# Attention and expert layers on one core: another order of the first loads, and identity multiplications in the first batch's attention

## The chip, the cores and the metric

The kernel runs on one core of a Trainium2 chip. The metric is the device time of one execution in microseconds (us). Engines are named as the profile names them: PE is TensorE (PEld its weight loads), DVE is VectorE, ACT is ScalarE, POOL is GpSimd, SP is the engine whose queue issues nearly all DMAs.

## The reference

```python
def sm_attn(qq, kk, vv):                       # softmax(q k^T / 8) v, row maximum subtracted
    s = scale * np.matmul(qq, kk.transpose(0, 1, 3, 2))
    ...
    return np.matmul(a, vv)
p_packed = sm_attn(p, k, v)                    # 32 packed queries per head, over 576 keys
out = sm_attn(q, p_packed, p_packed)           # 576 queries per head, over the 32 packed rows
# x = out with heads side by side: 4608 tokens x 512
p = domain_probs / (domain_probs.sum(-1, keepdims=True) + 1e-09)
for e in range(4):                             # w1[e] is 512 x 1024, w2[e] is 1024 x 512
    out += p[:, e:e + 1] * (np.maximum(x @ w1[e], 0.0) @ w2[e])
```

There are 8 batches of 8 heads with head dimension 64, all in float32; q, k and p are drawn eight times wider than usual.

## The kernel before

The expert layers are the bulk. Their 4096 hidden columns are cut into 8 chunks `ch` of 512. A unit (`units`, L332) is one chunk for one batch; there are 64, and the first four are chunk 0 and chunk 1 of batch 0, then chunk 0 and chunk 1 of batch 1. Each unit has a first product (hidden values, `mm1_part` and `mm1_evict`) and a second, which takes seven block products (`product`, in the order of `ORDER`) in place of eight. Between them DVE forms sums of blocks (`sblk`, L592), and every operand is split in a high part, which ACT casts, and a low part, which POOL subtracts (`s_operand`: tiles `st`, L110 and L114). The weights w2 of a chunk are split in the same way into seven pairs `tt` by `t_form` (sums at L633; casts and subtractions again at L110 and L114), are stored to DRAM (`td`, L610) and are loaded back for later batches (L606). A product needs the high and the low part of both its operands.

The attention output of a batch, split into `xh` and `xl`, is the moving operand of the first product. w1 is not multiplied with it directly: the packed values `ppbd` are folded into w1 first (`g_form`, and for batch 0 `folded`; operands `wraw`), and the result, split again, is `ghl`.

The start runs a path of its own for batch 0. Two `pack_unit` generators, one for each half `g` of the heads, make the packed values: scores of p and k (`scores`), row maximum and exponential, five transposes (L74), the products with v, one transpose of the result `ppn`, and copies to `ppbd`. Then `first_tokens` makes the scores of the 576 queries (operands `ppbd` and `kt`, here the tile of q), starts the fold of w1, does the softmax of the two halves in DVE and ACT, turns it (`turn`) and begins the first products. `fill` puts plain multiplications of the 128x128 identity by itself on PE, whose result is never read; there is one row of three, between the fold and the turn. `form` takes one step of `forms`, the generator that splits w2's chunk 0, and ties its cast to a place on ACT.

Batch 1's attention (`second`) runs between the products of units 0 and 1. Its last step is `xl` (POOL, L114), two of them, one for each half. Unit 2's first product needs both.

Within an engine the order is made by a scheduler from the order in which the code issues, except where `after` and `then` add an edge without a wait. SP issues DMAs strictly in its order, and an issue that waits holds all behind it.

Of the kernel before, what the change touches and what calls it, by code (L numbers as in the profile page):

```python
# [36 lines left out]
NPROD = len(ORDER)  # L37
FILL = (3,)


@with_exitstack
def attention_moe(ctx: ExitStack, tc: tile.TileContext, q, k, v, p, dp, w1, w2, out):
# [30 lines left out]
    def tr(**kw):  # L73
        on_pe(nc.tensor.transpose(**kw))  # L74
# [52 lines left out]

    def scores(bs, g, stationary, moving):

        pss = {b: dbl() for b in bs}  # L130
        calls = []
        for c in range(2):
            for j in range(2):
                for hh in range(2):
                    for b in bs:
                        p0 = 2 * j * NPK + cols(b, hh).start
                        calls.append(dict(
                            out=pss[b][p0:p0 + NPK, c, 0:HS], lhsT=stationary(b, 2 * g + j, hh),
                            rhs=moving[b][hh * D:(hh + 1) * D, j, c * HS:(c + 1) * HS], start=True, stop=True,
                        ))  # L140
        together(calls)
        return pss
# [6 lines left out]

    def pack_unit(bs, g, new, relief=False):  # L150
        nfull = S // P
# [19 lines left out]
        yield  # L171
        pss = scores(bs, g, lambda b, pr, hh: pts[b][hh * D:(hh + 1) * D, pr, :], kts)
        a1s, rss = {}, {}
# [24 lines left out]
        for b in bs:  # L198
            if b != bs[0]:
                vt = load_v(b)  # L200
            at = new(b, [P, len(SC), P], "at")
            ps = dbl()
            for c in range(nfull):
                tr(out=ps[:, 0, c * P:(c + 1) * P], in_=a1s[b][:, c * P:(c + 1) * P], identity=ident)
# [18 lines left out]
            yield  # L223
            ps = dbl()
            tr(out=ps[0:D, 0, 0:P], in_=ppn, identity=ident)
            psv = ps[0:D, 0, 0:P].rearrange("p (j n) -> p j n", j=2)
# [179 lines left out]
    def first_tokens(pools, qts, raws, forms, grps):  # L406
# [101 lines left out]
        last["ACT"] = marks["turned", b, 1]  # L508
        form()
        largest(0)  # L510
# [4 lines left out]
        scaled(0)  # L515
        form()
        form()
        spare = turned[0][:, 0, cut:cut + P]
        fill(FILL[0], spare)
        for g in range(NG):  # L520
            then("ACT", hi_of(ghls[g][:, 0, :], fold[:, g, :], nc.scalar))
        parts = turn(0)
        for g in range(NG):
            less(fold[:, g, :], ghls[g][:, 0, :])
        shifted(1)
        (t0, x0), (t1, x1) = parts
        then("DVE", hi_of(xh[:, 0, t0], x0, nc.vector))
        then("ACT", hi_of(xh[:, 0, t1], x1, nc.scalar))
        powers(1)
        for g in range(NG):  # L530
# [51 lines left out]
    def s_operand(u, i):  # L582

        name = ORDER[i] if u < LAST else PLAIN[i]
        blk = lambda n: blocks[u, n]
        if name[0] == "s":
            t = hpool.tile([P, 2, HS], F32, name="sblk", bufs=3)
            x, y, op = {
                "s1": ("a21", "a22", ALU.add), "s2": ("s1", "a11", ALU.subtract),
                "s3": ("a11", "a21", ALU.subtract), "s4": ("a12", "s2", ALU.subtract),  # L590
            }[name]
            marks["sum", u, name] = nc.vector.tensor_tensor(out=t, in0=blk(x), in1=blk(y), op=op).ins  # L592
            blocks[u, name] = t
        src = blk(name)
        st = st_tile(F32R)
        parts = hi_of(both(st, 0), src, nc.scalar).ins, lo_of(both(st, 1), src, both(st, 0), nc.gpsimd).ins
        for ins, prev in zip(parts, marks.get("operand", ())):
            after(ins, prev)
        marks["operand"] = parts
        blocks[u, "op", i] = st  # L600

# [12 lines left out]
    def t_form(ch, new, eng):  # L614
# [3 lines left out]
        for name, shape in (("b11", [P, 2, DH]), ("b12", [P, 2, DH]), ("b2", [P, 2, DM])):  # L618
            blk[name] = new(shape, name)
            r0 = hf * FC + (0 if name != "b2" else 2 * P)  # L620
            c0 = DH if name == "b12" else 0
            nc.sync.dma_start(
                out=blk[name], in_=w2[e, r0:r0 + 2 * P, c0:c0 + shape[2]].rearrange("(f p) d -> p f d", p=P),
            )
        blk["b21"], blk["b22"] = blk["b2"][:, :, 0:DH], blk["b2"][:, :, DH:DM]
        yield
# [146 lines left out]
    with ExitStack() as first:  # L773
# [5 lines left out]
        def form_tile(shape, name):  # L779
            if name == "b2":  # L780
                return st_tile(F32)[:, 0:2 * DM].rearrange("p (f d) -> p f d", f=2)
            return hpool.tile(shape, F32, name="ablk", bufs=6)

        packs = [pack_unit([0], g, unit_tile(g)) for g in range(NG)]
        forms = t_form(0, form_tile, {n: nc.gpsimd for n in ("t1", "t2", "t3", "t4")})
        norm_probs()
        for i in (0, 1, 0, 1):
            next(packs[i])
        loads = first_loads()
        qts = [next(loads)]  # L790
        next(forms)
        qts.append(next(loads))
        raws = w1_load(0)
        load_probs(0, 0)
# [18 lines left out]
    after(mm1_evict(0, *rest), marks["sum", 0, "s3"])  # L813
    drain(forms)

# [29 lines left out]
    for u, (sb, ch, b) in enumerate(units):  # L845
# [44 lines left out]
        for i in range(NPROD):  # L890
            product(u, i)
            if (u, i) == (0, 0):
# [3 lines left out]
                for raw, ghl in lows:  # L896
                    nc.scalar.copy(out=ghl[:, 1, :], in_=raw)
            n = i + LA
# [76 lines left out]
```

## Time and profile before

| | us |
|---|---|
| median of 3 runs (1280.68 to 1282.36) | 1282.11 |
| the profiled execution | 1287.0 |
| its span, first to last instruction | 1285.2 |
| PE busy in the span | 1264.0 (98%) |
| DVE / POOL / ACT busy | 955.6 / 859.9 / 492.0 |

The profile is of one execution. Busy PE time counts from the start of a matmul to its modelled end, so rows that overlap add up to more than the stretch they stand in, and a PE that is busy all the time can still be slow: its clock can be granted at half. [...] A multiplication of two float32 operands is two records in the profile, a transpose is one.

### The profile page before, as it was taken

The page shows a single profiled execution, that of the slowest core. Times are in us where ns is not written, and L with a number is a line of the kernel's source. Part 1 is how long each engine was busy: PE and PEld are TensorE (multiplying, and loading weights), DVE is VectorE, ACT ScalarE, POOL GpSimd, SP SyncE. Part 2 cuts the span into 40 slices and gives each one's busy share as a digit, 9 for nine tenths or more (in the row PEclk, how much of TensorE's full clock was granted, in tenths as well). Part 3 has the DMA queues.
Part 4 walks back from the last instruction along what each step waited for, and adds up shares of the span by engine and source line. Part 5 has one row for each costly group of instructions (what it writes and reads, how often), then busy time and mean ns, then how long its engine had stood idle before and what let it go on. Part 6 is the DMA issues. An engine that isn't in the chain of part 4 may idle for free.

```text
span 1285.2 us, 26859 instructions
## 1 busy us (share of the span) xinstructions
PE 1264.0 (98%) x10762; PEld 1177.1 (92%) x10762; DVE 955.6 (74%) x1299; ACT 492.0 (38%) x888; POOL 859.9 (67%) x570
## 2 busy tenths in 40 slices
PE   7999999999999999999999999999999999999998
PEld 5789998998999999999999999999999999999998
DVE  4686777899985666998677667799679567766776
ACT  2644535646335333333334423333333533332321
POOL 2878889798995455666578454476668755556565
PEclk7999999999999999999999999999999999999999
DMA  8896656545465444555355646434446443343563
GB/s 300 306 319 221 203 176 224 168 162 184 159 216 201 145 159 141 189 167 157 115 145 173 200 143 196 137 132 132 144 138 203 149 143 117 125 157 125 176 219 100
DMA packets 91707, 223.93 MB, mean 174 GB/s; under 512 B 9280, under 2 KB 32192, under 8 KB 91584
## 3 DMA queue, kind: packets, MB, share of 16 engines
q1 hardware_dynamic: 90768, 221.92, 52.2%
q8 instruction: 86, 1.41, 0.5%
q10 hardware_dynamic: 816, 0.30, 0.1%
q14 instruction: 37, 0.30, 0.1%
HBM read 183.31 MB, written 38.87 MB: 173 GB/s over the span
## 4 chain that ended last, share of the span: by engine, by line
PE 70%; POOL 15%; DVE 8%; issue 3%; DMA 2%; ACT 2%; SPq 0%; ACTq 0%; POOLq 0%; DVEq 0%
PE dbl L69 63%; POOL st L114 9%; PE dbl L79 6%; POOL tt L114 2%; DVE sblk L592 2%; POOL acc L743 2%; DVE ghl L114 1%; DVE acc L712 1%; DVE ablk L363 1%; POOL xl L114 1%; PE dbl L74 1%; DMA tt<-td 1%; ACT ghl L110 1%; POOL b L633 0%; DVE a L250 0%
## 5 line engine op out<-in xcount | busy, mean ns | idle before, releaser
L69 PE MATMUL dbl<-st,tt 128*128 128x288 f32 x5388 | 765.1, 296 | 4.3 <-DVE ghl L114 1.4
L69 PEld LDWEIGHTS dbl<-st,tt 128*128 128x128 f32 x5388 | 723.3, 188 | 49.1 <-issue 26.1
L114 POOL TENSOR_TENSOR st<-sblk,st 128x576 fp32r<-128x576 f32 x252 | 396.5, 1581 | 231.8 <-ACT st L110 227.0
L69 PE MATMUL dbl<-xh,ghl 128*128 128x288 f32 x2016 | 409.0, 295 | 2.2 <-DVE ghl L114 2.1
L114 POOL TENSOR_TENSOR st<-ablk,st 128x576 fp32r<-128x576 f32 x193 | 293.1, 1522 | 138.4 <-ACT st L110 133.2
L712 DVE TENSOR_TENSOR acc<-dbl,acc 128x576 f32<-128x576 f32 x385 | 287.5, 750 | 101.8 <-PE dbl L69 101.4
L69 PEld LDWEIGHTS dbl<-xh,ghl 128*128 128x128 f32 x2016 | 322.4, 188 | 3.0 <-DVE ghl L114 2.9
L363 DVE SCALAR_TENSOR_TENSOR ablk<-dbl,pbt 128x576 f32<-128x576 f32 x256 | 192.1, 752 | 141.3 <-PE dbl L69 138.9
L69 PE MATMUL dbl<-xl,ghl 128*128 128x288 f32 x1008 | 296.3, 295 | 0.2 <-POOL xl L114 0.2
L110 ACT CAST st<-sblk 128x576 fp32r<-128x576 f32 x252 | 170.2, 676 | 277.0 <-DVE sblk L592 222.3
L110 ACT CAST st<-ablk 128x576 fp32r<-128x576 f32 x193 | 130.2, 675 | 252.2 <-PE dbl L69 221.5
L69 PEld LDWEIGHTS dbl<-xl,ghl 128*128 128x128 f32 x1008 | 188.9, 188 | 0.5 <-POOL xl L114 0.5
L592 DVE TENSOR_TENSOR sblk<-ablk 128x576 f32<-128x576 f32 x126 | 134.9, 1071 | 9.6 <-DVE ablk L363 0.5
L110 ACT CAST ghl<-dbl 128x512 fp32r<-128x512 f32 x128 | 72.6, 587 | 117.9 <-PE dbl L79 60.1
L114 DVE TENSOR_TENSOR ghl<-dbl,ghl 128x512 fp32r<-128x512 f32 x124 | 83.3, 686 | 20.5 <-ACT ghl L110 18.5
L592 DVE TENSOR_TENSOR sblk<-ablk,sblk 128x576 f32<-128x576 f32 x63 | 77.5, 1230 | 5.4
L79 PE MATMUL dbl<-wraw,ppbd 64*32 64x512 f32 x1024 | 69.9, 604 | 0.0
L114 POOL TENSOR_TENSOR tt<-b,tt 128x512 fp32r<-128x512 f32 x42 | 62.8, 1504 | 2.1 <-ACT tt L110 2.0
L592 DVE TENSOR_TENSOR sblk<-sblk,ablk 128x576 f32<-128x576 f32 x63 | 57.6, 915 | 1.3
L743 POOL TENSOR_TENSOR acc<-acc,acc 128x576 f32<-128x576 f32 x28 | 43.4, 1561 | 12.5 <-DVE acc L712 12.5
L710 ACT COPY acc<-dbl 128x576 f32<-128x576 f32 x56 | 35.8, 640 | 36.8 <-PE dbl L69 36.8
L79 PEld LDWEIGHTS dbl<-wraw,ppbd 64*32 64x32 f32 x1024 | 15.3, 106 | 21.6 <-issue 19.2
(117 smaller groups left out, 474.3 us busy)
## 6 DMA issues: line engine op xcount, KB each, us to landing
tt<-td SPq DMA_DIRECT2D x192, 512.0 KB, 4.3
wraw<-in_w SPq DMA_DIRECT2D x136, 256.0 KB, 3.6
td<-tt SPq DMA_DIRECT2D x56, 512.0 KB, 3.9
pbt<-pnd SPq DMA_DIRECT2D x32, 288.0 KB, 4.0
out<-acc SPq DMA_DIRECT2D x31, 288.0 KB, 2.4
kt<-in_k SPq DMA_DIRECT2D x14, 576.0 KB, 5.6
kt<-in_q SPq DMA_DIRECT2D x14, 576.0 KB, 5.6
vt<-in_v SPq DMA_DIRECT2D x15, 512.0 KB, 5.4
```

The source lines that it names most:

```text
L69: res = nc.tensor.matmul(**kw)
L74: on_pe(nc.tensor.transpose(**kw))
L79: ins = nc.tensor.matmul(**kw).ins
L110: return nc.scalar.copy(out=dst, in_=src)
L114: return eng.tensor_tensor(out=dst, in0=src, in1=hi.bitcast(F32), op=ALU.subtract)
L363: res = nc.vector.scalar_tensor_tensor(out=a, in0=ps[:, :, 0:HS], scalar=0.0, in1=pbt[b][:, c * HS:(c + 1) * HS].rearrange("p (o t) -> p o ...
L592: marks["sum", u, name] = nc.vector.tensor_tensor(out=t, in0=blk(x), in1=blk(y), op=op).ins
L710: nc.scalar.copy(out=accs[b, i], in_=psv)
L712: nc.vector.tensor_tensor(out=accs[b, i], in0=psv, in1=accs[b, i], op=ALU.add)
L743: eng.tensor_tensor(out=m[dst], in0=m[x], in1=m[y], op=op)
```

## The change

First loads: SP loads both halves of q, then w1's chunk 0, then w2's chunk 0; before, w2's blocks stood between the first q and w1. w2's chunk 1 is now issued behind w1's chunk 1. w2's largest block (`b2`) of chunk 0 gets a tile of its own instead of borrowing one of the operand tiles.

Identity multiplications: nine ahead of the first scores of batch 0, two and four ahead of the transposes of its two halves, one ahead of each transpose of `ppn`; in `first_tokens` the row of three becomes a row of four ahead of the fold's correction by the high part (`less`), two ahead of the turn, which now comes behind that correction, and two ahead of the next correction.

Forms: of the seven steps that split w2's chunk 0, three are taken ahead of the first product and four behind the low parts of `ghl` in unit 0; before, all seven were taken ahead of the first product.

```diff
-FILL = (3,)
+FILL = (4, 2, 2)
+WARM = (9, 0, 2, 4, 0, 0, 1, 1)
...
+    def idle(ps, n):
+        return [dict(out=ps, lhsT=ident, rhs=ident, start=True, stop=True) for i in range(n)]
...
-        calls = []
+        calls = idle(pss[bs[0]][:, 1, HS:HS + P], fill)
...
+            if fill[1]:
+                together(idle(ps[:, 1, P:2 * P], fill[1]))
...
+            if fill[3]:
+                together(idle(ps[:, 1, 0:P], fill[3]))
...
-        form()
         largest(0)
...
-        form()
-        form()
-        spare = turned[0][:, 0, cut:cut + P]
-        fill(FILL[0], spare)
+        spare = accum[grps[0]][:, 1, HS:HS + P]
+        fill(FILL[0], turned[0][:, 0, cut:cut + P])
         for g in range(NG):
             then("ACT", hi_of(ghls[g][:, 0, :], fold[:, g, :], nc.scalar))
-        parts = turn(0)
         for g in range(NG):
             less(fold[:, g, :], ghls[g][:, 0, :])
+        form()
+        fill(FILL[1], turned[0][:, 0, cut:cut + P])
+        parts = turn(0)
         shifted(1)
...
+        fill(FILL[2], spare)
         powers(1)
...
+        if (u, i) == (0, 3):
+            after(parts[0], marks["lows"])
...
+            if ch == 1:
+                after(load.ins, marks["w1", 1])
...
-                return st_tile(F32)[:, 0:2 * DM].rearrange("p (f d) -> p f d", f=2)
+                return wpool.tile(shape, F32, name="b2")
...
-        loads = first_loads()
-        qts = [next(loads)]
+        qts = list(first_loads())
+        raws = w1_load(0)
         next(forms)
-        qts.append(next(loads))
-        raws = w1_load(0)
...
-    drain(forms)
...
                 for raw, ghl in lows:
-                    nc.scalar.copy(out=ghl[:, 1, :], in_=raw)
+                    last["ACT"] = nc.scalar.copy(out=ghl[:, 1, :], in_=raw).ins
+                marks["lows"] = last["ACT"]
+                for _ in forms:
+                    then("ACT", marks["form"])
...
-    nc = bacc.Bacc("TRN2", target_bir_lowering=False, num_devices=1)
+    nc = bacc.Bacc("TRN2", target_bir_lowering=False, num_devices=1, dynamic_dma_scratch_size=1024)
```

On PE the program starts so before (`kt,pt` are the scores of p and k, `ident,a` the transposes, `ppbd,kt` the scores of the queries, `wraw,ppbd` the fold, `ident,kt` the turn):

```order
L79 MATMUL dbl<-kt,pt 32x288 x16
L74 MATMUL dbl<-ident,a_215 128x128 x4
L74 MATMUL dbl<-ident,a_215 64x128
L74 MATMUL dbl<-ident,a_233 128x128 x4
L74 MATMUL dbl<-ident,a_233 64x128
L69 MATMUL dbl<-vt,at 32x64 x16
L69 MATMUL dbl<-vr,at 32x64 x4
L69 MATMUL dbl<-vt,at 32x64 x16
L69 MATMUL dbl<-vr,at 32x64 x4
L74 MATMUL dbl<-ident,ppn 64x128 x2
L79 MATMUL dbl<-ppbd_85,kt 128x64 x20
L79 MATMUL dbl<-wraw,ppbd_85 32x512 x8
```

and so with the change (the line numbers are its own):

```order
L80 MATMUL dbl<-ident 128x128 x9
L80 MATMUL dbl<-kt,pt 32x288 x16
L80 MATMUL dbl<-ident 128x128 x2
L75 MATMUL dbl<-ident,a_224 128x128 x4
L75 MATMUL dbl<-ident,a_224 64x128
L80 MATMUL dbl<-ident 128x128 x4
L75 MATMUL dbl<-ident,a_242 128x128 x4
L75 MATMUL dbl<-ident,a_242 64x128
L70 MATMUL dbl<-vt,at 32x64 x16
L70 MATMUL dbl<-vr,at 32x64 x4
L70 MATMUL dbl<-vt,at 32x64 x16
L70 MATMUL dbl<-vr,at 32x64 x4
```

Fifteen identity multiplications stand around the first batch's scores and transposes where there were none; two more follow, one ahead of each transpose of `ppn`.

On POOL the rows ahead of the first operand's low part are these before (`tt` the low parts of w2's chunk 0, L633 sums of w2's blocks, `st` low parts of product operands):

```order
L114 TENSOR_TENSOR tt<-ablk,tt 128x512
L633 TENSOR_TENSOR ablk<-ablk 128x512
L633 TENSOR_TENSOR ablk<-st_191,ablk 128x512
L114 TENSOR_TENSOR tt<-ablk,tt 128x512 x2
L633 TENSOR_TENSOR ablk<-st_191,ablk 128x512
L114 TENSOR_TENSOR tt<-ablk,tt 128x512
L633 TENSOR_TENSOR ablk<-ablk,st_191 128x512
L114 TENSOR_TENSOR tt<-ablk,tt 128x512
L114 TENSOR_TENSOR tt<-st_191,tt 128x512 x2
L114 TENSOR_TENSOR st_501<-ablk,st_501 128x2x288
```

and these with the change:

```order
L115 TENSOR_TENSOR tt<-ablk,tt 128x512
L646 TENSOR_TENSOR ablk<-ablk 128x512
L646 TENSOR_TENSOR ablk<-b_201,ablk 128x512
L115 TENSOR_TENSOR tt<-ablk,tt 128x512 x2
L646 TENSOR_TENSOR ablk<-b_201,ablk 128x512
L115 TENSOR_TENSOR st_515<-ablk,st_515 128x2x288
L115 TENSOR_TENSOR st_522<-sblk,st_522 128x2x288
L115 TENSOR_TENSOR st_568<-sblk,st_568 128x2x288
L115 TENSOR_TENSOR tt<-ablk,tt 128x512
```

Four low parts of w2's chunk 0 and one sum of its blocks have moved behind the first operand's low part.

Further on, POOL reaches batch 1's `xl` before over these rows (`a` is batch 1's softmax):

```order
L114 TENSOR_TENSOR st_997<-ablk,st_997 128x2x288
L114 TENSOR_TENSOR st_1019<-sblk,st_1019 128x2x288
L114 TENSOR_TENSOR tt<-b_523,tt 128x512
L114 TENSOR_TENSOR st_1066<-ablk,st_1066 128x2x288
L276 TENSOR_TENSOR a_852<-a_852,s_938 128x576
L114 TENSOR_TENSOR xl_807<-at,xh_806 128x576 x2
```

and with the change over these:

```order
L646 TENSOR_TENSOR b_527<-b_527,b_531 128x512
L115 TENSOR_TENSOR st_1088<-ablk,st_1088 128x2x288
L285 TENSOR_TENSOR a_874<-a_874,s_960 128x576
L115 TENSOR_TENSOR xl_829<-at,xh_828 128x576
L115 TENSOR_TENSOR tt<-b_527,tt 128x512
L115 TENSOR_TENSOR tt<-b_531,tt 128x512 x2
L115 TENSOR_TENSOR xl_829<-at,xh_828 128x576
```

Between the second operand's low part and the first `xl`, both included, POOL has 25 instructions before and 27 with the change. Three low parts of w2's chunk 1 now stand between the two `xl`.

## Rows read from the trace of the kernel before

**Rows 1.** The page: engines' share of the span, and the chain by engine.

```profile
PE 1264.0 (98%) x10762; PEld 1177.1 (92%) x10762; DVE 955.6 (74%) x1299; ACT 492.0 (38%) x888; POOL 859.9 (67%) x570
...
PE 70%; POOL 15%; DVE 8%; issue 3%; DMA 2%; ACT 2%; SPq 0%; ACTq 0%; POOLq 0%; DVEq 0%
```

**Rows 2.** Windows: PE, PEld, DVE, ACT, POOL busy, granted clock, DMA share, GB/s.

```profile
5.00:10.00 5.00, 4.42 (x37) 2.00 (x37) 1.51 (x5) 0.83 (x2) 0.00 (x0) 1.00 1.05 336
10.00:15.00 5.00, 3.67 (x87) 2.58 (x86) 1.92 (x7) 2.19 (x5) 1.12 (x1) 0.73 1.07 380
15.00:20.00 5.00, 4.84 (x25) 4.28 (x22) 1.15 (x5) 0.00 (x0) 2.68 (x3) 0.50 1.04 384
20.00:25.00 5.00, 5.00 (x27) 4.78 (x30) 1.85 (x3) 1.73 (x3) 1.36 (x2) 0.50 1.04 394
25.00:30.00 5.00, 5.00 (x26) 1.95 (x18) 4.31 (x6) 1.07 (x2) 2.39 (x2) 0.57 0.53 155
30.00:35.00 5.00, 3.70 (x23) 2.96 (x23) 2.66 (x5) 3.03 (x7) 0.77 (x1) 1.00 0.88 253
...
55.00:60.00 5.00, 5.00 (x106) 4.47 (x106) 2.95 (x6) 2.25 (x4) 5.00 (x4) 1.00 0.29 71
...
100.00:1285.00 1185.00, 1174.34 (x9990) 1105.17 (x9988) 892.91 (x1190) 448.26 (x806) 796.06 (x521) 1.00 0.50 163
```

**Rows 3.** Timeline of PE: start, length, engine, line, operands, records, wait before.

```profile
5.26 3.90 PE L79 MATMUL dbl<-kt,pt 64*32 64x288 f32 x32 [5.26 <-DMA kt<-in_k]
9.48 0.74 PE L74 MATMUL dbl<-ident,a 128*128 128x128 f32 x5 [0.33 <-ACT a L187]
...
12.24 1.08 PE L69 MATMUL dbl<-vt,at 128*32 128x64 f32 x32
...
13.62 1.08 PE L69 MATMUL dbl<-vt,at 128*32 128x64 f32 x32
...
16.01 8.77 PE L79 MATMUL dbl<-ppbd,kt 128*128 128x64 f32 x40
24.70 3.64 PE L79 MATMUL dbl<-wraw,ppbd 64*32 64x512 f32 x16
28.27 1.43 PE L79 MATMUL dbl<-ident 128*128 128x128 f32 x6
29.54 0.95 PE L79 MATMUL dbl<-ident,kt 128*128 128x128 f32 x5
...
41.01 1.92 PE L79 MATMUL dbl<-wraw,ppbd 64*32 64x512 f32 x16
...
45.10 1.17 PE L79 MATMUL dbl<-xh,pt 64*32 64x288 f32 x16
...
52.02 1.25 PE L74 MATMUL dbl<-ident,a 128*128 128x128 f32 x10
...
56.38 0.65 PE L69 MATMUL dbl<-vt,at 128*32 128x64 f32 x32
...
57.21 0.65 PE L69 MATMUL dbl<-xl,kt 128*32 128x64 f32 x32
```

**Rows 4.** Timeline of ACT, the high parts of the fold.

```profile
28.44 1.07 ACT L110 CAST ghl<-dbl 128x512 fp32r<-128x512 f32 x2 [4.36 <-PE dbl L79]
```

**Rows 5.** Timeline of POOL, from the second operand's low part to both `xl`.

```profile
44.74 2.79 POOL L114 TENSOR_TENSOR st<-sblk,st 128x576 fp32r<-128x576 f32 x2 [1.47 <-ACT st L110]
...
62.22 1.27 POOL L114 TENSOR_TENSOR tt<-b,tt 128x512 fp32r<-128x512 f32 x1 [1.28 <-ACT tt L110]
...
81.69 1.43 POOL L114 TENSOR_TENSOR xl<-at,xh 128x576 fp32r<-128x576 f32 x1
84.72 1.43 POOL L114 TENSOR_TENSOR xl<-at,xh 128x576 fp32r<-128x576 f32 x1 [1.60 <-ACT xh L110]
```

**Rows 6.** Timeline of PE around the first `xl`.

```profile
83.18 0.40 PE L69 MATMUL dbl<-xl,ghl 128*128 128x288 f32 x1 [0.24 <-POOL xl L114]
...
90.52 1.92 PE L79 MATMUL dbl<-wraw,ppbd 64*32 64x512 f32 x16
```

More of the change, by code (lines that the diff above doesn't have):

```diff
@@ L126, in norm_probs, with scores @@
         nc.scalar.dma_start(out=pnd.rearrange("e (p t) -> p e t", p=P), in_=pb)
-    def scores(bs, g, stationary, moving):
+    def idle(ps, n):
+        return [dict(out=ps, lhsT=ident, rhs=ident, start=True, stop=True) for i in range(n)]
+    def scores(bs, g, stationary, moving, fill=0):
         pss = {b: dbl() for b in bs}
-        calls = []
+        calls = idle(pss[bs[0]][:, 1, HS:HS + P], fill)
         for c in range(2):
@@ L148, in behind_w1, with pack_unit @@
             after(res.ins, marks["w1", 1])
-    def pack_unit(bs, g, new, relief=False):
+    def pack_unit(bs, g, new, relief=False, fill=(0, 0, 0, 0)):
         nfull = S // P
@@ L171, in pack_unit @@
         yield
-        pss = scores(bs, g, lambda b, pr, hh: pts[b][hh * D:(hh + 1) * D, pr, :], kts)
+        pss = scores(bs, g, lambda b, pr, hh: pts[b][hh * D:(hh + 1) * D, pr, :], kts, fill[0])
         a1s, rss = {}, {}
@@ L621, in t_form @@
             c0 = DH if name == "b12" else 0
-            nc.sync.dma_start(
+            load = nc.sync.dma_start(
                 out=blk[name], in_=w2[e, r0:r0 + 2 * P, c0:c0 + shape[2]].rearrange("(f p) d -> p f d", p=P),
             )
+            if ch == 1:
+                after(load.ins, marks["w1", 1])
         blk["b21"], blk["b22"] = blk["b2"][:, :, 0:DH], blk["b2"][:, :, DH:DM]
@@ L780, in form_tile @@
             if name == "b2":
-                return st_tile(F32)[:, 0:2 * DM].rearrange("p (f d) -> p f d", f=2)
+                return wpool.tile(shape, F32, name="b2")
             return hpool.tile(shape, F32, name="ablk", bufs=6)
-        packs = [pack_unit([0], g, unit_tile(g)) for g in range(NG)]
+        packs = [pack_unit([0], g, unit_tile(g), fill=WARM[g::NG]) for g in range(NG)]
         forms = t_form(0, form_tile, {n: nc.gpsimd for n in ("t1", "t2", "t3", "t4")})
```

## The prediction

> **What bounds the kernel now.** I read the page's shares and its chain first: PE is busy for 98% of the span and holds 70% of the chain, POOL 15% [rows 1]. So a microsecond counts only where PE stands still, runs slowly or does work it needn't. The windows came next, for the clock. From 100 us on PE is busy for 1174.3 of 1185.0 us at full clock, and the change leaves the order there nearly as it was, so nothing is to be had there [rows 2]. [...] In 30 to 35 us it was busy for 3.70 of 5 us and kept the full clock [rows 2].
>
> The scores of k ran at half speed too, whatever the window shows there: 32 records in 3.90 us, while 16 records of the same shape take 1.17 us later [rows 3].
>
> Then I read the timeline of POOL from the second operand's low part on, because PE waits for POOL at 83.18 us, for the first `xl` [rows 5, 6]. POOL is busy without a break in 55 to 60 us [rows 2], and from 44.74 to the end of that `xl` at 83.12 its only long wait that I found is the 1.28 us at 62.22 [rows 5]. There POOL and PE finish together. This place decides what an earlier start is worth.
>
> **The front, part by part.** I add up how much earlier PE starts the turn (29.54 before) if the clock rises early and stays.
>
> Nine identity rows: an identity multiplication at half clock costs two records of 0.21 us (six records fill 28.27 to 29.54) [rows 3], so nine cost 3.8 us. PE has nothing else until k lands at 5.26 [rows 3], and the identity is ready at the program's start, so they are hidden; if the tile were late, up to 3.8 us would be in front of the scores.
>
> Scores of k: 16 records take 2.0 us cold and 1.17 warm; the second half of them waits for its load anyway, so I take 0.9 us (bounds 0 and 1.0). Of this only 0.3 reaches the products with v, because DVE now copies the first half's transposed rows behind the second half's reciprocal, which waits for ACT's exponential; the copy and that product are queued behind it.
>
> Products with v: the two sets start 1.38 us apart at half clock and 0.83 apart at full clock [rows 3], so two sets give 1.1. The two and four rows before the transposes lie in PE's waits for ACT and DVE, the one before each `ppn` transpose behind DVE's scaling; at 0.21 each at full clock I cost them at nothing, and 1.7 us for all eight if that cover is gone.
>
> Query scores: 40 records take 8.77 us, 0.219 each [rows 3]. The trace has none of them at full clock. Bounds: 4.4 us if all of it follows the clock, 8.77 if nothing does. The nearest rows are the transposes with as wide a weight tile at full clock, ten in 1.25 us, 0.125 each including the tail [rows 3], 5.0 us for 40. I take 4.4, since the tail is there once.
>
> Fold: 3.64 becomes 1.92 as at 41.01 [rows 3], so 1.7. w1's arrival: p, k, v, q and w1 are 4.65 MB, and at 336 to 394 GB/s [rows 2] this is there by about 16 us; PE now wants it at about 19. The old order with w2's 1.05 MB first would have made it just in time, so the new order of loads I count as nothing; if it were late the cost is at most the 2.7 us of those bytes.
>
> Between fold and turn: 1.2 us before (28.34 to 29.54). Now ACT's two casts (1.07 [rows 4]) and four rows (0.85) run side by side, then the second correction (0.3) and two rows (0.43) come before the turn: 1.8. That loses 0.6. DVE's softmax of the first half has the turn's operand ready some 0.5 us sooner, by the same chain as before.
>
> Sum: 0.3 + 1.1 + 4.4 + 1.7 - 0.6 = 6.9; I take 6.8 us. Bounds: 7.5, and -1.4 if no clock is gained. From the turn to the second operand's low part the same instructions follow in the same order at full clock; the two rows before the next correction lie beside DVE's copy of `xh`. So that low part starts at 44.74 - 6.8 = 37.9.
>
> **What is given back.** Three of w2's seven splits are taken ahead of the first product, four and one sum behind it; three low parts of the next chunk have moved past the first `xl`. From the second operand's low part to the first `xl` POOL has 27 instructions where it had 25. In the profile 25 took 38.4 us, 37.1 without the wait at 62.22: 1.486 each [rows 5]. 27 are 40.1 us (bounds: 41.5 with the waits as before; 36, if every one had the shortest time for its kind). The first `xl` is done at 78.0, where PE at its own pace would have wanted it near 76. POOL idles earlier, before the first product, where those five used to stand; that idle time can't be had back.
>
> PE waits for `xl` at that point with more left to do: of the two products that stood ahead of it before, ten records each now stand behind. From the first `xl` to the next fold PE had 54 records in 7.34 us, 0.136 each [rows 6]; now 76, 10.3 us, and some 0.3 of waiting for the second `xl`, three low parts later. So that fold starts at 78.0 + 10.6 = 88.6 instead of 90.5. Gain: 1.9 us. Everything behind it is bound by PE and is moved by the same amount. The loads of w2's chunk 1, now queued on SP behind w1's and ahead of batch 1's v, hold back nothing that PE wants before 50 us; the smaller scratch and the tile of `b2` add no instruction that the order shows.
>
> The profiled execution is 1287.0 us, its span 1285.2 and 1.8 around it; the sum makes it 1285.1. The median of the timed runs is 4.9 lower, and I subtract from it: 1282.1 - 1.9 = **1280.2**.
>
> **Rivals.** *POOL is no bound* (1275.6). If the low parts run at their shortest and PE finds other work, nearly all 6.8 is kept, less 0.3. For it: POOL waits for ACT here and there, so its times hold slack. Against: PE already waits for `xl` before.
>
> *The clock falls again* (1286.9). Around the transposes PE has gaps still; if the rows in them don't do, it falls as before, and the products with v, the scores and the fold run as before, while added rows cost. Scores start about 0.6 earlier, the fold ends at 27.8, the turn stays within 0.1 of its place, and POOL then takes 40.1 us from 44.6: the next fold is at 95.3, 4.8 late. It is slower from the point where the front gains less than about 4.9 us, since POOL asks for that much. For it: the gaps, and the half clock in 15 to 25 us with PE busy throughout [rows 2]. Against: in 30 to 35 us gaps did no harm.
>
> *The weight loads don't follow the clock* (1284.6). In 15 to 25 us the weight loads are busy for 4.28 and 4.78 of 5 us [rows 2]: the scores are bound by them. If 0.219 us per record stays, the front gains 2.4, and 44.74 - 2.4 + 40.1 + 10.6 = 93.0, 2.5 late. [...] Against: transposes with 128 columns of weights ran at 0.125 per record at full clock [rows 3]. [...]
>
> *It does nothing*: more waits on POOL use up the rest, 1282.
>
> **Chances.** Forecast 0.50 (its own range 1277.5 to 1283), POOL no bound 0.13, clock falls 0.20, weight loads 0.09, nothing 0.08. What a measurement here can tell from no change is about 0.2%, 2.6 us: faster is under 1279.5, slower over 1284.7. The forecast gives 0.18 to faster, 0.31 to same and 0.01 to slower; POOL no bound gives 0.13 to faster; clock 0.17 to slower and 0.03 to same; weight loads 0.04 and 0.05; nothing 0.02 and 0.06. Together 0.31, 0.45, 0.24. The range from 1276.0 to 1286.5 leaves out most of the second case and half of the third.
>
> **What the profile will show.** If right: a granted clock that rises in 5 to 9 us and stays at 1.00 through 29; query scores at about 0.11 us a record; the turn near 22.7 and the first fold behind the products' start near 34; POOL without a break from 38 to 83; PE waiting some 5 us in sum for POOL ahead of the first `xl`, near 72 to 78. Wrong would be a clock of 0.5 anywhere in 12 to 29 us, scores at over 0.16 a record with full clock, or an `xl` that PE doesn't wait for.

## The result

The changed kernel takes 1286.91 us, median of 7 runs (1286.38 to 1293.53). The kernel before, timed beside it, takes 1280.70 (7 runs, 1280.36 to 1282.36). The ratio is 1.0053, with a 95% interval of 1.0040 to 1.0065: slower by 6 us, where the prediction said 1280.2 and kept 1286.5 as the end of its range.

The profiled execution of the changed kernel is 1286.91 us, span 1285.1, just its median. That of the kernel before was 1287.0, span 1285.2. So by the two profiles alone nothing has happened, and by the timed runs 6 us were lost. This is the first thing to explain.

The page, shares and chain:

```profile
PE 1264.4 (98%) x10806; PEld 1180.6 (92%) x10806; DVE 955.3 (74%) x1299; ACT 492.7 (38%) x888; POOL 859.3 (67%) x570
...
PE 72%; POOL 12%; DVE 9%; issue 3%; ACT 2%; DMA 1%; SPq 0%; ACTq 0%; POOLq 0%; DVEq 0%
```

PE has 44 records more, two for each of 22 added identity multiplications; the chain reads nearly as in [rows 1]. The windows of the changed kernel, columns as in [rows 2]:

```profile
5.00:10.00 5.00, 4.66 (x49) 2.76 (x49) 1.99 (x6) 0.83 (x2) 0.00 (x0) 1.00 1.08 340
10.00:15.00 5.00, 4.04 (x98) 2.98 (x97) 2.37 (x10) 1.57 (x4) 0.00 (x0) 1.00 1.04 386
15.00:20.00 5.00, 5.00 (x48) 4.63 (x52) 2.34 (x4) 0.69 (x1) 0.00 (x0) 1.00 0.97 292
20.00:25.00 5.00, 4.85 (x39) 3.00 (x29) 3.54 (x7) 1.59 (x3) 1.80 (x2) 1.00 0.99 328
...
100.00:1285.00 1185.00, 1174.53 (x9984) 1105.91 (x9982) 891.51 (x1190) 448.31 (x805) 795.26 (x520) 1.00 0.50 164
```

Where [rows 2] has 0.73, 0.50 and 0.50, the granted clock is now 1.00. Behind 100 us PE is busy for 1174.5 of 1185 us, as before. Its timeline, to set against [rows 3, 6]:

```profile
14.85 4.65 PE L80 MATMUL dbl<-ppbd,kt 128*128 128x64 f32 x40 [0.25 <-PE dbl L75]
19.43 1.92 PE L80 MATMUL dbl<-wraw,ppbd 64*32 64x512 f32 x16
...
23.58 0.95 PE L80 MATMUL dbl<-ident,kt 128*128 128x128 f32 x5
...
35.05 1.92 PE L80 MATMUL dbl<-wraw,ppbd 64*32 64x512 f32 x16
...
63.54 4.98 PE L70 MATMUL dbl<-st,tt 128*128 128x288 f32 x36 [0.80 <-DVE a L259]
69.42 0.53 PE L70 MATMUL dbl<-st,tt 128*128 128x288 f32 x2 [0.90 <-POOL st L115]
71.16 2.77 PE L70 MATMUL dbl<-st,tt 128*128 128x288 f32 x10 [1.22 <-POOL tt L115]
...
78.44 0.53 PE L70 MATMUL dbl<-st,tt 128*128 128x288 f32 x2 [2.51 <-ACT tt L111]
...
79.61 0.31 PE L70 MATMUL dbl<-xl,ghl 128*128 128x288 f32 x1
...
89.95 1.92 PE L80 MATMUL dbl<-wraw,ppbd 64*32 64x512 f32 x16
```

The turn starts at 23.58 instead of 29.54 and the first product's fold at 35.05 instead of 41.01: the front did win 6 us against the profiled execution. Then PE waits for DVE, POOL and ACT in turn, 5.4 us in the rows shown, and the second fold starts at 89.95, only 0.57 earlier than in [rows 6]. The ten records at 71.16 take 2.77 us where twelve take 1.8 elsewhere: from 70.8 to 74.2 us the granted clock is 0.50. It falls in the second of the waits that end at 69.42 and 71.16. It is 0.50 once more from 320 to 323.4. POOL, to set against [rows 5]:

```profile
38.78 2.79 POOL L115 TENSOR_TENSOR st<-sblk,st 128x576 fp32r<-128x576 f32 x2 [2.79 <-ACT st L111]
41.54 1.80 POOL L115 TENSOR_TENSOR tt<-ablk,tt 128x512 fp32r<-128x512 f32 x1
...
51.36 4.29 POOL L115 TENSOR_TENSOR tt<-b,tt 128x512 fp32r<-128x512 f32 x3
...
78.04 1.43 POOL L115 TENSOR_TENSOR xl<-at,xh 128x576 fp32r<-128x576 f32 x1
79.42 3.79 POOL L115 TENSOR_TENSOR tt<-b,tt 128x512 fp32r<-128x512 f32 x3
83.16 1.44 POOL L115 TENSOR_TENSOR xl<-at,xh 128x576 fp32r<-128x576 f32 x1
```

It starts its row 6 us earlier than in [rows 5] and ends the first `xl` at 79.47, 3.65 earlier; between the two `xl` stand three low parts.

### The profile page after: what moved, and what is told of

The parts are those of the page before. It is cut to its first block, busy times and chain, and to the rows that moved or that the text cites. A ratio compares the mean times of both kernels' runs of the same rounds, so it can differ in the third digit from the quotient of the medians.

```text
span 1285.1 us, 26939 instructions
## 1 busy us (share of the span) xinstructions
PE 1264.4 (98%) x10806; PEld 1180.6 (92%) x10806; DVE 955.3 (74%) x1299; ACT 492.7 (38%) x888; POOL 859.3 (67%) x570
## 4 chain that ended last, share of the span: by engine, by line
PE 72%; POOL 12%; DVE 9%; issue 3%; ACT 2%; DMA 1%; SPq 0%; ACTq 0%; POOLq 0%; DVEq 0%
PE dbl L70 66%; POOL st L115 8%; PE dbl L80 6%; DVE sblk L601 2%; POOL acc L756 2%; DVE ghl L115 1%; DVE acc L725 1%; DVE ablk L372 1%; POOL tt L115 1%; PE dbl L75 1%; ACT ghl L111 1%; POOL xl L115 1%; DVE a L259 1%; DVE m L264 0%; POOL b L646 0%
## 5 line engine op out<-in xcount | busy, mean ns | idle before, releaser
L80 PEld LDWEIGHTS dbl<-wraw,ppbd 64*32 64x32 f32 x1024 | 15.2, 106 | 21.1 <-issue 19.5
```

Of the source, the lines that this page charges most:

```text
L80: ins = nc.tensor.matmul(**kw).ins
```

## The experiments

Theory 1: the mechanics of the prediction are right, but the profiled execution of the kernel before is not what its timed runs usually do; these have no long stretch of half clock, so the front had nothing to win, and what is left is the price of the low parts put behind the first product. Theory 2: before is cold (at a granted clock of 0.50 in its front) in all runs, and the new falls of the clock at 70.8 and 320 us, or the rows, cost the time. All timings are in one table at the end of this section. In these runs the kernel before falls on levels of its own, so beside the medians I give the lowest time of each kernel; the lowest of the kernel before stays within 1280.1 and 1280.4 on every chip.

**The kernel before once more** (no edit).

> The kernel before, unchanged. The one profile of it lay 4.9 us above the median of the timed runs then at hand, and shows half clock from 12.3 to 29.3 us. Theory 1 (the timed runs mostly lack that cold stretch, so the identity rows had nothing to win): its time is 1280 to 1282 us and its new profile shows a mean clock of 0.997 or more, with the query scores near 0.12 us a record. Theory 2 (before is cold in all its runs, and the change loses its time elsewhere): the profile again shows half clock until 29 us, mean clock 0.993.

1280.46, and its profile is one of 1280.37 (span 1278.6). PE there:

```profile
5.17 4.07 PE L79 MATMUL dbl<-kt,pt 64*32 64x288 f32 x32 [5.17 <-DMA kt<-in_k]
9.39 1.30 PE L74 MATMUL dbl<-ident,a 128*128 128x128 f32 x5 [0.16 <-ACT a L187]
11.46 0.77 PE L74 MATMUL dbl<-ident,a 128*128 128x128 f32 x5 [0.76 <-ACT a L187]
...
14.70 4.77 PE L79 MATMUL dbl<-ppbd,kt 128*128 128x64 f32 x40
19.40 2.02 PE L79 MATMUL dbl<-wraw,ppbd 64*32 64x512 f32 x16
...
34.29 1.92 PE L79 MATMUL dbl<-wraw,ppbd 64*32 64x512 f32 x16
...
83.78 1.92 PE L79 MATMUL dbl<-wraw,ppbd 64*32 64x512 f32 x16
```

The scores of k still run at half pace (32 records in 4.07 us), and so do the first five transposes (1.30 us, the next five 0.77). From 11.5 us on everything is at full pace: the query scores take 4.77 us and not 8.77, the fold behind the turn starts at 34.29 and not 41.01, the second fold at 83.78 and not 90.52. That is 6.74 us, and the two executions differ by 6.6. In the profiles of this study (but for the last kernel's, 1196.1) the time from the second fold to the end of the span lies between 1194.4 and 1195.8 us, so where that fold starts tells the kernel's time to a microsecond or so. Without any of the added identity rows the usual run of before has its first fold 0.76 us *ahead* of the changed kernel's 35.05. The first fold thus ends the front. From there to the second fold before takes 49.49 us here and 49.51 in [rows 3, 6], the changed kernel 54.90: 5.4 us are lost behind the first fold. The table at the end gives this stretch for every kernel. Theory 1 holds in its first half, theory 2 falls there.

**The rows alone.** `packs = [pack_unit([0], g, unit_tile(g), fill=WARM[g::NG]) ...]` and the code for it, nothing else of the change.

> Before with the identity rows ahead of the first scores and among the first batch's attention steps alone; loads, low parts and turn as before. Theory 1: the front is full clock in both, so 1279 to 1282 us. If the cold stretch is in before's timed runs, it gains 5 us: 1276. Theory 2 (more identity work brings later stretches of half clock): slower, 1283 to 1287, with falls of the clock near 70 and 320 us in its profile.

1283.89, slower by 2 us than before. The profile has a wait for the second query load, and after it the clock's lower level:

```profile
18.51 4.07 PE L80 MATMUL dbl<-ppbd,kt 128*128 128x64 f32 x20 [1.50 <-DMA kt<-in_q]
22.52 3.53 PE L80 MATMUL dbl<-wraw,ppbd 64*32 64x512 f32 x16
```

Sixteen fold records in 3.53 us, against 1.92, are at half pace; the granted clock is 0.50 in 20 to 25 us. So the rows bring the full clock at 5.5 us (the first 16 records of the scores of k take 1.17 us there) instead of about 11, and it is lost again behind the wait for that load. Why the load lands later than in before is open. Behind the first fold nothing is lost (49.52 us); theory 1's "same" is missed by 2 us, and so is theory 2's fall at 70 us.

**The early low parts with all the rest of the change.**

```diff
+        form()
         largest(0)
...
         scaled(0)
+        form()
+        form()
...
-        form()
         fill(FILL[1], turned[0][:, 0, cut:cut + P])
...
     after(mm1_evict(0, *rest), marks["sum", 0, "s3"])
+    drain(forms)
...
-                for _ in forms:
-                    then("ACT", marks["form"])
```

> The changed kernel, with the low parts of the second layer's first operand formed at the places where before has them, instead of behind the first product. Theory 1 (the late low parts cost, by POOL's row from 38 to 83 us): 1279 to 1282 us, as before or a little faster. Theory 2: no gain from it, 1286 to 1288.

1285.04, between the two. PE's two folds:

```profile
38.84 1.92 PE L80 MATMUL dbl<-wraw,ppbd 64*32 64x512 f32 x16
...
88.34 1.92 PE L80 MATMUL dbl<-wraw,ppbd 64*32 64x512 f32 x16
```

Between them lie 49.50 us, as in before: with early low parts the rest of the change loses nothing behind the first fold. What this kernel loses, it loses ahead of it (38.84 against 34.29), and there a third thing shows. ACT, start and wait of the first cast of w2, and of the next two:

```profile
18.09 0.62 ACT L111 CAST tt<-ablk 128x512 fp32r<-128x512 f32 x1 [5.89 <-DMA ablk<-in_w]
...
23.04 1.14 ACT L111 CAST tt<-ablk 128x512 fp32r<-128x512 f32 x2 [3.62 <-POOL ablk L648]
24.08 1.06 ACT L111 CAST ghl<-dbl 128x512 fp32r<-128x512 f32 x2
```

With w2 loaded behind w1, the casts on ACT wait for it, and the cast that the fold's correction needs stands behind them in ACT's order. PE waits 3.14 us for it at 25.20 and then runs at half pace for some three microseconds (granted clock 0.66 in 25 to 30), and the turn, which the change puts behind that correction, starts at 26.77. So with early low parts the new load order and the moved turn together cost 4.6 us in the front.

**The change without the rows.** `FILL = (3, 0, 0); WARM = (0,) * 8`.

> The changed kernel without any of the added identity rows (the one row of three that before has is kept); loads and low parts as changed. Theory 1: as slow as the changed kernel or slower by what the front loses, 1286 to 1291 us. Theory 2 (the rows and the later falls of the clock cost the time): 1280 to 1283.

1288.88, lowest 1286.92, as theory 1 says: the loss stays without the rows. Against the kernel before beside each, the ratios are 1.0054 without the rows and 1.0053 with them, so neither a gain nor a cost of the rows is shown here.

**The late parts alone**: before, with its loads, and

```diff
-        form()
         largest(0)
...
-        form()
-        form()
         spare = turned[0][:, 0, cut:cut + P]
...
         for g in range(NG):
             less(fold[:, g, :], ghls[g][:, 0, :])
+        form()
...
-                return st_tile(F32)[:, 0:2 * DM].rearrange("p (f d) -> p f d", f=2)
+                return wpool.tile(shape, F32, name="b2")
...
-    drain(forms)
...
+                for _ in forms:
+                    then("ACT", marks["form"])
```

> The kernel before with one part of the change: the remaining low parts of the second layer's first operand formed behind the first product (own tile for b2, smaller DMA scratch with it); loads and identity rows as before. Theory 1 (late low parts cost by POOL's row): the fold ahead of the first product stays where the usual profile of before has it (34.3 us), the second fold comes near 90 us instead of 83.8, and the time is 1285 to 1289. Theory 2 (only late loads with late parts cost): 1280.4 to 1282.

1286.54: the whole loss, with before's loads and no added row. First fold 34.15, second 90.39:

```profile
34.15 1.92 PE L79 MATMUL dbl<-wraw,ppbd 64*32 64x512 f32 x16
...
68.50 0.53 PE L69 MATMUL dbl<-st,tt 128*128 128x288 f32 x2 [0.91 <-POOL st L114]
70.25 1.58 PE L69 MATMUL dbl<-st,tt 128*128 128x288 f32 x10 [1.22 <-POOL tt L114]
...
76.34 0.53 PE L69 MATMUL dbl<-st,tt 128*128 128x288 f32 x2 [2.66 <-ACT tt L110]
...
90.39 1.92 PE L79 MATMUL dbl<-wraw,ppbd 64*32 64x512 f32 x16
```

The waits are those of the changed kernel.

**The load order alone**, low parts early:

```diff
+            if ch == 1:
+                after(load.ins, marks["w1", 1])
...
-        loads = first_loads()
-        qts = [next(loads)]
+        qts = list(first_loads())
+        raws = w1_load(0)
         next(forms)
-        qts.append(next(loads))
-        raws = w1_load(0)
```

> The kernel before with the changed load order alone (queries, w1, w2; the second chunk's w2 behind w1), low parts formed where before forms them. Theory 1: the casts of the low parts' operand on ACT wait for w2, which lands some 3 us later, and hold up the cast ahead of the turn, as in the run with early parts and rows (turn 25.2 instead of 23.5): 1283 to 1286. If the order costs nothing by itself: 1280.4 to 1282.

1282.16, ratio 1.0007 (0.9995 to 1.0019): unclear, at most a small loss. Its profile has 1.27 us of PE waiting for the same cast on ACT, for a correction that starts at 24.96, nearly where it does with early parts and rows (25.20; the expectation calls that the turn). But here the turn stands ahead of the correction, at 22.68, and the first fold is at 34.77. So early low parts bear the new load order as long as the turn doesn't wait for that cast. The profiled execution is one of 1283.38, above the median; it has half clock from 58.2 to 61.6 us (0.82 in 55 to 60, 0.84 in 60 to 65) and is 2.3 us above the kernel's lowest run, so its 52.32 us between the folds may not be typical.

**`b2`'s own tile and the smaller scratch alone** (of the diff of the late parts only the line on `b2`):

> The kernel before with only b2's own tile and the smaller DMA scratch, which both runs with late parts carry along. Theory 1: no effect, 1280.3 to 1282. If they cost: above 1283, and the loss of the late parts has to be read against it.

1281.89 against 1281.86: nothing. The loss is the low parts.

**Both query loads ahead of w2**, without and with rows (`qts = list(first_loads()); next(forms)`):

> The kernel before with both query loads ahead of the w2 loads, w1 still behind w2, no added rows. If the queries' second half sets the front, it gains up to 0.5 us in most runs, and the spread to 1286.8 goes: 1279.5 to 1281. If w2 (for ACT's casts) is then late: 1282 to 1284.

> The same with the identity rows ahead of the first scores and in the first batch's attention. In the run with the rows alone the second half of the queries landed 1.5 us late and the clock fell behind it. Theory 1 (the front is set by loads and the ACT and DVE chain, not by the clock): with the queries in time, no wait there and no fall, 1279 to 1281.5, no better than without the rows by more than 0.5. Theory 2 (rows bring falls by themselves): 1283 to 1286.

1281.76 and 1281.28, both the same as before. With the queries in time the rows do no harm, and with equal records at full pace from 5.2 us on the second fold still starts at 83.80 (83.78 in the usual run of before). The 0.4 us that the rows win ahead of the query scores are gone by the end of the fold: it takes 2.54 us instead of 2.02, both kernels start the identity rows behind it at 21.35, and in both the turn then waits for DVE (0.47 and 0.48 us). With rows:

```profile
83.80 1.92 PE L80 MATMUL dbl<-wraw,ppbd 64*32 64x512 f32 x16
```

The profile without rows fell on an execution of 1281.81 and shows what that level is:

```profile
11.63 1.33 PE L74 MATMUL dbl<-ident,a 128*128 128x128 f32 x5 [0.76 <-ACT a L187]
12.89 1.08 PE L69 MATMUL dbl<-vt,at 128*32 128x64 f32 x32
...
14.27 0.85 PE L69 MATMUL dbl<-vt,at 128*32 128x64 f32 x32
```

Here both rows of transposes and the first products with v run at half pace too, and full pace begins only within the second set of products (0.85 us, between 1.08 and 0.65). That costs 1.5 us: the first fold is at 35.77, the second at 85.28.

**Why the low parts cost 6 us.** Theory 1 has POOL's row for it. Two kernels were to shake that: the late low parts on DVE (below), and only two of them late (in before, only the drain moved, with `b2`'s own tile).

```diff
-            lo_of(t[:, 1], blk[n], t[:, 0], nc.gpsimd)
+            lo_of(t[:, 1], blk[n], t[:, 0], nc.vector if ch == 0 and i > 2 else nc.gpsimd)
```

> The changed kernel, with the low parts of the four late tiles formed on DVE instead of POOL (some 0.69 us each there instead of 1.28). Theory 1 (the loss is POOL's row between the first product and the first low query part): POOL gets some 5 us back, PE's waits between 62 and 79 us shrink, and the time is 1281 to 1284. Rival (the loss is the lateness of the tiles itself, or the clock): unchanged, 1286 to 1288.

> The kernel before with only the last two low parts and no sum behind the first product (the run with all four and the sum lost 6 us); own tile for b2 and smaller DMA scratch as there. Theory 1: POOL has about 2.5 us more behind the first product against 6.4, less the slack of some 1 to 3 us that before's row has there: 1281 to 1283. Rival (a step, that any late tile costs the whole): 1286.

1285.94 and 1287.42: POOL's sum alone fails. In both, PE's waits for POOL in 62 to 79 us are gone, and others have come (late parts on DVE):

```profile
75.02 1.82 PE L70 MATMUL dbl<-st,tt 128*128 128x288 f32 x12 [1.51 <-DVE acc L725]
77.66 0.66 PE L70 MATMUL dbl<-xh,ghl 128*128 128x288 f32 x3 [0.33 <-DVE ghl L115]
81.10 1.82 PE L70 MATMUL dbl<-st,tt 128*128 128x288 f32 x12 [0.68 <-DVE acc L725]
```

Windows of 60 to 80 us, in order: before as usual, late parts on POOL, on DVE, two of them late (PE, PEld, DVE, ACT, POOL busy):

```profile
60.00:80.00 20.00, 19.73 (x145) 17.50 (x145) 14.42 (x25) 8.18 (x14) 17.81 (x13) 1.00 0.95 325
```
```profile
60.00:80.00 20.00, 13.46 (x92) 10.89 (x92) 17.02 (x26) 9.94 (x17) 18.73 (x14) 0.96 0.64 226
```
```profile
60.00:80.00 20.00, 17.68 (x140) 14.24 (x133) 18.20 (x27) 8.71 (x16) 18.47 (x14) 1.00 0.92 338
```
```profile
60.00:80.00 20.00, 17.67 (x141) 14.25 (x134) 18.19 (x26) 8.69 (x16) 19.59 (x14) 1.00 0.76 270
```

POOL has 2 us to spare in the first, DVE 5.6. In the last two DVE is up to 18.2 of 20: the second chunk's two sums on DVE, at 46.64 and 52.88 in the usual run, stand at 54.13 and 59.44 with two parts late, because the difference they need comes behind the late parts on POOL (51.93 instead of 45.33). The profiles also say how much each costs behind the first fold, where before takes 49.5 us: two late parts 3.3 us, late parts on DVE 4.2, four and a sum on POOL, without the rows, 6.7. So half the parts cost about half. That the kernel with two is no faster has another reason in its profiled execution: the granted clock is 0.50 from 11.8 to 15.2 us (a set of its products with v takes 1.08 us, not 0.65), and its first fold comes 1.3 us late (35.63). Its other five runs are slower still, and no trace shows why.

**The second chunk's tiles later** was to empty that stretch (`(3, 5) if u == 0 else (0, 1, 2, 3, 5) if u == 1`), in the changed kernel, in before, and in the version with rows and adjacent queries:

> The changed kernel, with the second chunk's tiles formed later: two of them in the first unit instead of four (behind products 3 and 5), five in the second. Theory 1b (between 40 and 80 us POOL is busy without a break and DVE nearly so; whatever is added there pushes out the second tokens' softmax and its low parts): two low parts and a sum or two leave that stretch, some 4 us of POOL and 2 of DVE, and 2 to 5 us come back: 1282 to 1285. Rival (the late tiles cost by being late themselves): 1286 to 1288.

> The same edit on the kernel before. PE's waits between 36 and 90 us sum to 1.4 us in its usual profile. Theory 1b: at most 1.4 us to gain: 1279 to 1282. If work that lands in the second unit is not covered there: 1283 or more.

> The same edit on the kernel before with identity rows and both query loads ahead of w2. Theory 1b: as the run above, 1279 to 1282, with fewer runs at 1286.8; it would be the best of all if the edit gains anything.

1286.77, 1281.97 and 1282.43. The first tells nothing: POOL's order in 36 to 90 us came out as it was, 46.0 us busy in both. The other two are the same as before. None beats it.

**The work taken away.** First the late low parts off every compute engine: this kernel leaves the four out and copies another tile's low part in their place. Then the second chunk's sums off DVE: this one leaves two subtractions out, and with them the edge that held one behind batch 1's softmax (`after(op, marks["bias", 1, 1])`), so its products are of the wrong blocks.

```diff
+            if ch == 0 and i > 2:
+                nc.sync.dma_start(
+                    out=t[:, 1].rearrange("p f d -> p (f d)").bitcast(F32),
+                    in_=tt[0, 0][:, 1].rearrange("p f d -> p (f d)").bitcast(F32),
+                )
+            else:
+                lo_of(t[:, 1], blk[n], t[:, 0], nc.gpsimd)
```

```diff
-                op = eng[m].tensor_tensor(out=blk[place], in0=blk[x], in1=blk[y], op=ALU.subtract).ins
-                if ch == 1 and m == "t3":
-                    after(op, marks["bias", 1, 1])
                 blk[m] = blk[place]
+                if ch == 1 and m in ("t2", "t3"):
+                    continue
+                eng[m].tensor_tensor(out=blk[place], in0=blk[x], in1=blk[y], op=ALU.subtract)
```

> The changed kernel with the four late low parts not computed: a copy by DMA of the first tile's low part stands in their place (casts, sum and products stay). Theory 1b (it is the work in the rows of POOL and DVE): POOL gets 5.1 us back, the second chunk's sums on DVE come some 5 us earlier, and the time falls to 1280.5 to 1283. Rival (the tiles' lateness, or the casts' order on ACT): 1285 to 1288.

> The changed kernel without the two subtractions on DVE for the second chunk's tiles (left out, the tiles take the uncombined blocks). If POOL's row sets the second tokens' low parts: the same, 1286 to 1288. If DVE's row does: 2.9 us leave its full stretch, and the time falls to 1283 to 1285.

1283.49 and 1285.51. The lowest is 4.2 us under the changed kernel's in the first case and 1.6 in the second; between the folds they take 51.37 and 52.61 us, against 54.90. So the four low parts (41.0 us of POOL busy in 36 to 90, against 46.0) are most of the loss. That run doesn't keep the tiles as late as they were, since the copies are issued at 32.4 to 44.5 us and take 6.4 us in the median to land, while POOL forms the parts from 41.54 to 55.65. But lateness by itself is ruled out in the changed kernel: its timeline shows no wait on PE between 30.89 and 62.7 us, and all seven products with the first chunk's tiles start there (36.90 to 59.31). Leaving two sums out on DVE, with POOL's row left nearly as it was (45.7 us busy against 46.0), helps a little too; whether by DVE's time or by the missing edge is open. PE in the first of them:

```profile
72.11 1.81 PE L70 MATMUL dbl<-st,tt 128*128 128x288 f32 x12 [0.99 <-DVE acc L728]
75.24 0.80 PE L70 MATMUL dbl<-xh,ghl 128*128 128x288 f32 x4 [1.31 <-ACT xh L111]
...
86.62 1.92 PE L80 MATMUL dbl<-wraw,ppbd 64*32 64x512 f32 x16
```

What it still waits for is DVE and ACT. How the 5.4 us of the changed kernel divide among POOL, DVE and ACT no run separates.

The last column is from each profile: us from the start of the first fold (behind the first product's start) to that of the second.

| kernel | median | lowest | before beside it | ratio, 95% | fold to fold |
|---|---|---|---|---|---|
| before, once more | 1280.46 | 1280.17 | 1281.73 | 0.9970 to 0.9999 | 49.49 |
| changed | 1286.91 | 1286.38 | 1280.70 | 1.0040 to 1.0065 | 54.90 |
| rows only | 1283.89 | 1281.81 | 1281.73 | 1.0005 to 1.0028 | 49.52 |
| changed, early low parts | 1285.04 | 1283.32 | 1281.73 | 1.0015 to 1.0038 | 49.50 |
| changed, no rows | 1288.88 | 1286.92 | 1281.73 | 1.0033 to 1.0075 | 56.27 |
| late low parts only | 1286.54 | 1285.77 | 1280.64 | 1.0031 to 1.0056 | 56.24 |
| load order only | 1282.16 | 1281.07 | 1280.64 | 0.9995 to 1.0019 | 52.32 |
| queries adjacent | 1281.76 | 1280.15 | 1280.64 | 0.9994 to 1.0015 | 49.51 |
| the same with rows | 1281.28 | 1280.38 | 1280.64 | 0.9993 to 1.0012 | 49.51 |
| late low parts on DVE | 1285.94 | 1285.71 | 1281.86 | 1.0033 to 1.0059 | 53.66 |
| two late only | 1287.42 | 1285.96 | 1281.86 | 1.0038 to 1.0062 | 52.77 |
| own tile only | 1281.89 | 1280.22 | 1281.86 | 0.9988 to 1.0015 | 49.50 |
| changed, second chunk later | 1286.77 | 1286.22 | 1281.86 | 1.0028 to 1.0055 | 54.92 |
| before, second chunk later | 1281.97 | 1281.20 | 1281.86 | 0.9985 to 1.0014 | 50.32 |
| rows, adjacent, second chunk later | 1282.43 | 1280.72 | 1281.86 | 0.9982 to 1.0010 | 50.32 |
| changed, late low parts copied | 1283.49 | 1282.16 | 1281.98 | 0.9994 to 1.0018 | 51.37 |
| changed, no second sums on DVE | 1285.51 | 1284.76 | 1281.98 | 1.0014 to 1.0037 | 52.61 |

## Why the prediction was wrong

The step that failed is one sentence: "The median of the timed runs is 4.9 lower, and I subtract from it". The gain was worked out on an execution whose front was cold (granted clock 0.50 [rows 2]) from 12.3 to 29.3 us, and subtracted from runs that mostly are not. Of 146 timed executions of the kernel before, 65 lie at 1280.1 to 1281.1, 52 at 1281.4 to 1282.4, and 16 at 1286.6 to 1287.5 (13 between). Profiles show the three: full pace from 11.5 us on and no fall; half pace until about 14.5 us (read from a kernel that differs only in the order of two loads); and the fall of [rows 2], which lasts until 29.3. The prediction's profile was of the rarest. The 4.9 us between it and the median were the front's loss, already absent from the median. They could have been asked about before anything was taken from it, since 4.9 is of the size of the whole claimed front. For a run without that loss the prediction's own sum has no gain in front, and behind it the 4.9 us that it gives back there (6.8 less 1.9): a loss of nearly the measured size.

The miss is 6.7 us: 4.9 by that step; 1.35 because the second fold started at 89.95 and not 88.6; 0.5 behind that fold.

Point by point, against the profiled execution of before:
- Clock: right. It rose near 5.5 us (from there 32 records of the scores of k take 2.40 us, 3.90 in [rows 3]) and stayed at 1.00 through 29. That it would fall near 71 us, in the waits for POOL, was not seen; the kernel with late parts only loses as much without half clock in that place (ten records in 1.58 us).
- Query scores: 4.65 us for 40, 0.116 each at a granted clock of 1.00 against 0.219 at 0.50, where 4.4 us were forecast. Their loads of weights follow the clock in these two traces: the median of 40 is 0.192 us with the change, at 1.00, and 0.333 before, at 0.50, so the rival by which they don't is out. Changed kernel, then before (ns, least, median, most):

```profile
L80 PEld LDWEIGHTS dbl<-ppbd,kt x40: 186/192/192, 14.8 to 19.2; 128*128 128x128 f32 x40
```
```profile
L79 PEld LDWEIGHTS dbl<-ppbd,kt x40: 289/333/334, 16.0 to 24.3; 128*128 128x128 f32 x40
```

- Turn 23.58 against 22.7, a gain of 6.0 instead of 6.8: from the fold's end to the turn it took 2.2 us, not 1.8, and the scores started 0.2 later and took 0.2 more.
- POOL's row: 40.7 us from 38.78 to the end of the first `xl`, against 40.1 from 37.9; `xl` done at 79.47 against 78.0. PE from the first `xl` to the fold: 10.3 us, as forecast. The size of this part was right, and it is the loss: "slower from the point where the front gains less than about 4.9 us" held, with a front that in the usual run gained nothing (its fold 0.76 later than before's 34.29).
- POOL as the only bound was too simple. Of PE's 5.4 us of waits ahead of the first `xl` 2.1 are put down to POOL; the prediction had them all there. The `xl` itself, at 79.61, PE doesn't wait for, which the prediction had named as a sign of being wrong: the last wait, 2.51 us, is put down to a cast on ACT. With the low parts on DVE most of the loss stayed.
- The load order at nothing: true for w1. But it takes the early places from the low parts, which the prediction took as a given of the change and not as a price of the order.

The rival "the clock falls again" gave 1286.9, the time that was measured, by a mechanism that did not happen: the front kept the full clock. That agreement is luck.

## What to carry to other kernels

When the profiled execution and the median differ by as much as the gain in question, find the stretch where they differ first: a stall that is in the profile and not in most runs is not there to be won. Work moved out of a stretch where its engine idles into one where two engines are nearly full is paid for there, whatever the front shows: 5.4 us here, with POOL busy for 18.7 and DVE for 18.8 of the 20 us from 60 to 80. And before a row of filler instructions is added, ask what sets the pace behind it: here the rows raised the clock some 6 us earlier (equal records at full pace from 5.2 us instead of 11.5), and the second fold started where it did without them (83.80 and 83.78).

## What was not expected of the hardware

- One program has three levels: 1280.4, 1281.9 and 1286.9 us (their medians). The nine profiles of kernels whose PE runs the same first 12 us as before (no added rows) differ in when the clock rises. In five the first five transposes, at 9.3 to 9.5 us, take 1.00 to 1.30 us and the next five 0.77: the clock rose among them or just behind and stayed through the front. In three they take 0.74, so it had risen earlier, and after a wait of 1.3 us it fell at 11.7 to 12.3; it was back at about 15 in two and at 29.3 in [rows 2]. In one it rose at about 14.5. What sets the moment of the rise, no run here shows.
- The window's clock column reads 1.00 in 5 to 10 us where 32 records of scores take 4.07 us, and 2.40 us in the changed kernel where the clock had been raised; it reads 1.00 also in 10 to 15 us of the execution whose products with v took 1.08 us instead of 0.65. At the start of these runs the pace of equal records tells the clock, not that column.
- One operation of 128x512 on DVE took 0.68 us while POOL waited, and another 1.88 when it started 0.1 us behind one of POOL's (and the sum that takes 0.68 below took 1.91 in before as usual, 0.07 us behind one), so the parts moved from POOL to DVE, at 1.20, 1.88 and 3.45 us for two, cost more than the 0.69 us each that were expected. DVE, then POOL, of the kernel with late parts on DVE (start, length):

```profile
47.74 1.88 DVE L115 TENSOR_TENSOR tt<-ablk,tt 128x512 fp32r<-128x512 f32 x1 [2.32 <-ACT tt L111]
...
54.99 0.68 DVE L646 TENSOR_TENSOR ablk<-b,ablk 128x512 f32<-128x512 f32 x1
```
```profile
47.64 1.43 POOL L115 TENSOR_TENSOR st<-ablk,st 128x576 fp32r<-128x576 f32 x1
...
56.41 1.28 POOL L115 TENSOR_TENSOR tt<-ablk,tt 128x512 fp32r<-128x512 f32 x1 [2.14 <-ACT tt L111]
```

POOL's operation ends at 49.07 and DVE's at 49.62, 0.55 later. What makes DVE's the longer one beside POOL's, these rows don't show.
